# Batch 0 of a fused pooled-attention and feed-forward kernel: other PSUM banks for four steps, and one step earlier in TensorE's queue

## The chip, the cores and the metric

The kernel runs on one core of one Trainium2 chip. The metric is the time of one execution on the device in microseconds; 291.48 us is the median of three executions of the kernel before (291.36 to 291.85). One more execution was taken with the hardware profiler, and all rows below come from it.

## The reference, cut to what matters

```python
batch, n_heads, seq, head_dim = (8, 8, 576, 64)      # q, k, v
k_p = k.reshape(B, H, Sp, pool, D).mean(axis=3)      # pool = 8, Sp = 72
v_p = v.reshape(B, H, Sp, pool, D).mean(axis=3)
scores = scale * np.matmul(q, k_p.transpose(0, 1, 3, 2))
attn = np.exp(scores - max) / (sum + 1e-09)
attn_out = np.matmul(attn, v_p)
x = attn_out.transpose(0, 2, 1, 3).reshape(B * S, H * D)   # 4608 x 512
h = x @ w_in                                               # 512 x 2048
out = (h * np.cos(h)) @ w_out                              # 2048 x 512
```

Attention over keys and values pooled by eight, and behind it a feed-forward layer whose activation is h cos(h).

## The kernel before, in words

The work goes through nine chunks of 512 tokens (`TILE`). Each of the eight batches has 576 tokens: 512 make the chunk of the batch, and the last 64 of every batch together make the ninth chunk. For each chunk the feed-forward part multiplies by `w_in` (`up_mm`, L357), takes the cosine on ScalarE (`up_g`, L364), multiplies on VectorE (L367) and multiplies by `w_out` (`down_mm`, L370). The attention of batch b + 1 is worked in between the matmuls of the down-projection of chunk b. Batch 0 has nothing to hide behind: its attention is the prologue of the kernel, from L495 to L538, and this is what the diff changes.

PSUM is laid out by hand: three tiles `banks[0]` to `banks[2]` of two banks each (a bank is 512 float32 columns of 128 partitions) and two tiles `obanks[0]` and `obanks[1]` of one bank each. Every engine works through its own instructions in the order in which the program writes them (`manual_schedule`), and waits on semaphores where it reads what another engine writes, or writes what another still reads. These waits are made for whole banks: a read of columns 256 to 511 waits for an earlier write to columns 0 to 255 of the same bank.

The steps of batch 0, with the lines under which the profile lists them:

- `pool_k_mm` (L180) pools k by matmuls with the 0/1 matrix `groups`; copies L186 put the result into `kk`.
- `q_transpose_mm` (L240) transposes q in blocks; copies L241 put it into `qT`.
- `scores` is `scores_mm` (L260) and `scores_exp` (L270). A unit `us[i]` is 256 tokens by 4 heads: us[0] and us[1] are the two token halves for heads 0 to 3, us[2] and us[3] for heads 4 to 7. `REST` is the last 64 tokens for all heads, "the last columns".
- `sums_mm` (L289) sums the exponentials over keys by matmuls with `ones`; `inverse` is a logarithm (L304) and an exponential of its negative (L305) on ScalarE.
- `pool_v_mm` (L196) pools v of four heads; its `put` (L205) copies the result into `vz` on VectorE.
- `values_mm` (L298) multiplies pooled v by a unit's exponentials; `x_mul` (L312) multiplies the result by the inverse sums into `xT`, which `up_mm` reads. The first eight `up_mm` matmuls need heads 0 to 3 only, the next eight heads 4 to 7.
- `warm_up` (L487) is matmuls on constant data whose result nobody reads.

v of batch 0 comes in two transfers of 288 KB as bfloat16, heads 0 to 3 and heads 4 to 7, started by GpSimd at 3.03 and 3.84 us; q, k and the weights come by the same queue. ScalarE's work for this batch ends with the exponentials of `REST` (L270, `ex_rest`), and then it loads the tables for the cosine (L348).

Of the kernel before, what the change touches and what calls it, by code (L numbers as in the profile page):

```python
# [19 lines left out]
def kernel(  # L20
# [9 lines left out]
    nc = tc.nc  # L30
    B, H, S, D = q.shape
    Sp = S // POOL
# [14 lines left out]
    REST = (SEG[2], (0, H))  # L47
# [29 lines left out]
    banks = [psum.tile([128, 2, 512], FP32, name=f"bank{i}") for i in range(3)]  # L77
    obanks = [psum.tile([128, 512], FP32, name=f"obank{i}") for i in range(2)]
# [70 lines left out]
    def v_part(b):  # L149
        return vz[b % 2][:, :, 0:4:3, :]  # L150
# [39 lines left out]
    def pool_v_mm(b, pair, j0, j1):  # L190
        vb = staged["v", b]
        n = (j1 - j0) * D
        ps = pair if isinstance(pair, tuple) else (pair[:, 0, :], pair[:, 1, :])
        for t in range(ROW):
            for hp, rows in enumerate(half):
                nc.tensor.matmul(ps[hp][:Sp, 0:n], lhsT=groups[rows, t, :], rhs=vb[rows, j0:j1, t, :],  # L196
                                 start=(t == 0), stop=(t == ROW - 1))
        dst = v_part(b)[:, j0:j1].rearrange("p j a d -> p a j d")

        def put():  # L200
            parts = [(dst[:, a], p[:Sp, 0:n]) for a, p in enumerate(ps)]
            if not isinstance(pair, tuple):
                parts = [(dst, pair[:Sp, :, 0:n])]
            for o, i in parts:
                nc.vector.tensor_copy(out=o, in_=i.rearrange("p (j d) -> p j d" if o is not dst else "p a (j d) -> p a j d", d=D))  # L205

        return put

# [15 lines left out]
    def qT_tile(b):  # L224
        att["qT", b] = asb.tile([128, QB, 128], BF16, name="qT", tag="qT")

    def q_flat(b):
        return staged["q", b].rearrange("p j t d -> p (j t d)")
# [5 lines left out]
    def q_transpose_mm(b, bank, g0, g1):  # L234

        if ("qT", b) not in att:
            qT_tile(b)
        ps = bank.bitcast(BF16)[:, 0:(g1 - g0) * 128].rearrange("p (g n) -> p g n", n=128)
        for g in range(g0, g1):
            nc.tensor.matmul(ps[:, g - g0, :], q_flat(b)[:, g * 128:(g + 1) * 128], identity, is_transpose=True)  # L240
        return lambda copy: copy(out=att["qT", b][:, g0:g1, :], in_=ps)  # L241

    def ex_col(u, i):

        (c0, n), (h0, nh) = u
        return (i // 2 % 2 * (nh // 2) + i // 4 * 2 + i % 2) * n

    def scores(b, u, pair):
        scores_mm(b, u, pair)
        scores_exp(b, u, pair)  # L250

    def scores_mm(b, u, pair):
        (c0, n), (h0, nh) = u

        for i in [i + 2 * a for k in range(0, nh, 4) for i in (k, k + 1) for a in range(2)]:
            bank, c = divmod(ex_col(u, i), nh * n // 2)
            pj, hp = divmod(h0 + i, 2)
            g, r = divmod(ROW * pj + ORDER[c0 // 64], 2)
            ps = pair[bank][:Sp, c:c + n] if isinstance(pair, tuple) else pair[:Sp, bank, c:c + n]
            nc.tensor.matmul(ps.rearrange("p (g n) -> p g n", n=64),  # L260
                             lhsT=kk[b % 2][half[r], h0 + i, 0:Sp],
                             rhs=att["qT", b][half[r], g:g + n // 64, hp * 64:hp * 64 + 64])

    def scores_exp(b, u, pair):
        (c0, n), (h0, nh) = u
        ex = ex_rest[b % 2] if u == REST else asb.tile([Sp, 4 * 256], BF16, name="ex", tag="ex", bufs=EX)
        w = nh * n // 2
        for src, c, m in ([(pair[:Sp, :, 0:w], 0, 2)] if not isinstance(pair, tuple) else
                          [(bank[:Sp, 0:w].unsqueeze(1), a * w, 1) for a, bank in enumerate(pair)]):
            nc.scalar.activation(out=ex[:, c:c + m * w].rearrange("p (a n) -> p a n", a=m), in_=src,  # L270
                                 func=ACTF.Exp, scale=scale / POOL)
        att["ex", b, u] = ex

    def token(b, c0):

        return b * TILE + c0 if c0 < TILE else B * TILE + b * 64

    def quads(u):

        (c0, n), (h0, nh) = u  # L280
        for i in range(nh):
            yield i, (h0 + i) // 4, slice((h0 + i) % 4 * 32, (h0 + i) % 4 * 32 + 32), slice(ex_col(u, i), ex_col(u, i) + n)

    def sums_mm(b, u, cs):

        ex = att["ex", b, u]
        q0 = u[1][0] // 4
        for i, q, rows, c in quads(u):
            nc.tensor.matmul(cs[rows, q - q0, :], lhsT=ones[:Sp, :], rhs=ex[:, c])  # L289

    def values_mm(b, u, ps):

        ex = att.pop(("ex", b, u))
        q0 = u[1][0] // 4
        for e in range(2):
            for i, q, rows, c in quads(u):
                pj, hp = divmod(u[1][0] + i, 2)
                nc.tensor.matmul(ps[rows, q - q0, e, :],  # L298
                                 lhsT=vz[b % 2][:, pj, 3 * hp, :].rearrange("p (d e) -> p e d", e=2)[:, e],
                                 rhs=ex[:, c])  # L300

    def inverse(cs, name, bufs):
        inv = asb.tile([128] + list(cs.shape[1:]), FP32, name=name, tag=name, bufs=bufs)
        nc.scalar.activation(out=inv, in_=cs, func=ACTF.Ln)  # L304
        nc.scalar.activation(out=inv, in_=inv, func=ACTF.Exp, scale=-1.0)  # L305
        return inv

    def x_mul(b, q, c0, ps, inv):

        n = ps.shape[3]  # L310
        c = token(b, c0)
        nc.vector.tensor_mul(out=xT[:, :, q, c:c + n], in0=ps[:, 0], in1=inv.unsqueeze(1).to_broadcast([128, 2, n]))  # L312
# [108 lines left out]
    def first_q(copy, t0, t1):  # L421
        copy(out=q01[:, t0 * D:t1 * D], in_=first[:, 1, t0 * D:t1 * D])
# [18 lines left out]
    groups = consts.tile([128, ROW, Sp], BF16, name="groups")  # L441
# [42 lines left out]
    def warm_up(n, bank):  # L484

        for i in range(n):
            nc.tensor.matmul(bank, lhsT=warm[:, 0:128], rhs=warm)  # L487

    vec, act = nc.vector.tensor_copy, nc.scalar.copy
    us = BY_HEADS  # L490

    def unit(bank):
        return bank.rearrange("p (q e n) -> p q e n", q=1, e=2)

    warm_up(8, banks[1][:, 0, :])  # L495
    puts = pool_k_mm(0, obanks, 0, 2)
    warm_up(2, banks[1][:, 0, :])
    first_q(act, 0, 7)
    first_q(vec, 7, 18)
    puts[0](vec)  # L500
    puts[1](act)
    q_transpose_mm(0, banks[2][:, 0, :], 5, 9)(act)
    q_transpose_mm(0, banks[0][:, 0, :], 0, 5)(vec)
    warm_up(2, banks[1][:, 0, :])
    scores(0, us[0], banks[0])
    scores(0, us[1], banks[1])
    for put in pool_k_mm(0, obanks, 2, 4):
        put(vec)
    s01 = banks[0][:, 0, :].rearrange("p (i n) -> p i n", i=2)
    sums_mm(0, us[0], s01[:, 0:1])  # L510
    puts = q_transpose_mm(0, banks[2][:, 0, :], 9, 14), q_transpose_mm(0, banks[2][:, 1, :], 14, 18)
    for put in puts:
        put(vec)
    sums_mm(0, us[1], s01[:, 1:2])
    inv01 = inverse(banks[0][:, 0, :], "inv", 1)
    warm_up(1, obanks[0])
    scores(0, us[2], banks[2])
    scores(0, us[3], banks[1])
    pool_v_mm(0, tuple(obanks), 0, 2)()
    for i in range(2):  # L520
        values_mm(0, us[i], unit(banks[0][:, i, :]))
    s23 = [ob[:, 256:512] for ob in obanks]
    sums_mm(0, us[2], s23[0].unsqueeze(1))
    put = pool_v_mm(0, banks[2], 2, 4)
    scores_mm(0, REST, tuple(obanks))
    x_mul(0, 0, 0, unit(banks[0][:, 0, :]), inv01[:, 0:256])
    put()
    x_mul(0, 0, 256, unit(banks[0][:, 1, :]), inv01[:, 256:512])
    sums_mm(0, us[3], s23[1].unsqueeze(1))
    for i in range(2):  # L530
        values_mm(0, us[2 + i], unit(banks[2][:, i, :]))
    for i in range(2):
        inv = inverse(s23[i], "inv_h", 2)
        x_mul(0, 1, 256 * i, unit(banks[2][:, i, :]), inv)
    scores_exp(0, REST, tuple(obanks))
    bk = banks
    up_mm(0, 0, 0, 2)
    up_mm(0, 1, 0, 2)  # L538
# [9 lines left out]
    for t in range(NT):  # L548
        b = t + 1
        bk = [banks[1], banks[0], banks[2]] if t == 1 else banks  # L550
        for fp in range(FFCH // 2):
            up_mm(t, fp, 2 if fp < 2 and t < 1 else 0)
            between = ()
            if t == 0:
                if fp == 6:
                    puts = q_transpose_mm(1, obanks[0], 0, 5), q_transpose_mm(1, obanks[1], 5, 9)
# [70 lines left out]
        elif b < B:  # L627
            us = BY_TOKENS
# [4 lines left out]
            d = 2 if t == 1 else 0  # L633
# [84 lines left out]
```

## Time and profile before

| | |
|---|---|
| median of three executions | 291.48 us |
| their range | 291.36 to 291.85 us |
| the profiled execution's own time | 291.54 us |
| its span, first to last instruction | 289.5 us |
| granted TensorE clock, mean over the span | 0.997 |
| TensorE (PE) busy | 278.9 us, 96% of the span |
| VectorE (DVE) busy | 170.5 us, 59% |
| ScalarE (ACT) busy | 142.7 us, 49% |
| GpSimd (POOL) busy | 145.5 us, 50% |
| first up-projection matmul (L357) starts | 15.69 us |

Times inside the profile count from the span's start. A row of a timeline has the start, the busy time, the engine, the line, the operation, what is written and read, shapes, and a count where several were merged; in square brackets stands how long the engine had been idle before it and what ended that. TensorE's matmuls overlap one another, and the end of each is modelled, so that a row's busy time reaches into the next row. Some matmul records are missing from the trace.

### The profile page before, as it was taken

What the parts mean: (1) busy time and instruction counts of PE and PEld (TensorE: products, weight loads), DVE (VectorE), ACT (ScalarE), POOL (GpSimd) and SP (SyncE); (2) the same over time, 40 slices, a digit from 0 to 9 for tenths busy, and PEclk for the clock granted to TensorE, in tenths of its full rate; (3) what the DMA queues carried; (4) which work ended last, traced back from release to release, by engine and by line L of the source; (5) the groups of instructions that cost most, each with busy time, mean ns of one, the idle gap of its engine ahead of it and who ended that gap; (6) DMA issues with size and microseconds to landing.
All of it is one profiled execution on the core that took longest, in us unless ns stands there. A gap on an engine that the chain in (4) does not pass through costs nothing.

```text
span 289.5 us, 4905 instructions
## 1 busy us (share of the span) xinstructions
PE 278.9 (96%) x1955; PEld 146.7 (51%) x1989; DVE 170.5 (59%) x231; ACT 142.7 (49%) x143; POOL 145.5 (50%) x121
## 2 busy tenths in 40 slices
PE   7899999999999999999999999999999999999994
PEld 3655544555554555555555545554555454445443
DVE  6467886664756564757375737583766467217621
ACT  4786634678056904691369326841676065016400
POOL 8546937999964696479544983698000000000000
PEclk9999999999999999999999999999999999999998
DMA  7999999789877978795879776965603510230033
GB/s 204 197 205 211 206 206 191 150 155 217 134 149 104 202 118 168 103 162 111 171 73 202 114 155 114 188 122 112 130 1 74 119 36 2 56 83 8 0 72 74
DMA packets 57158, 36.89 MB, mean 127 GB/s; under 512 B 36400, under 2 KB 50928, under 8 KB 57136
## 3 DMA queue, kind: packets, MB, share of 16 engines
q0 software_dynamic: 17104, 17.77, 37.9%
q1 hardware_dynamic: 39792, 18.69, 32.7%
q8 instruction: 15, 0.25, 0.3%
q10 hardware_dynamic: 240, 0.13, 0.2%
q14 instruction: 7, 0.06, 0.1%
HBM read 36.70 MB, written 9.44 MB: 159 GB/s over the span
## 4 chain that ended last, share of the span: by engine, by line
PE 90%; DVE 3%; ACT 2%; DMA 2%; issue 1%; SPq 0%; DVEq 0%
PE bank L357 40%; PE obank L370 25%; PE bank L370 7%; PE obank L376 5%; PE bank L260 3%; PE bank L329 3%; PE bank L376 2%; DVE g_sb L367 2%; DMA g_sb<-in_q_dram 2%; ACT cos L364 2%; PE bank L398 1%; ACT ex L270 1%; PE bank L298 1%; DVE qT L241 0%; PE bank L240 0%
## 5 line engine op out<-in xcount | busy, mean ns | idle before, releaser
L364 ACT ACTIVATE cos<-bank,half_pi 128x1024 f32<-128x1024 f32 x72 | 80.4, 1118 | 117.3 <-PE bank L357 116.1
L357 PE MATMUL bank<-xT,w_in_sb 128*128 128x512 bf16 x565 | 125.4, 379 | 0.6
L367 DVE TENSOR_TENSOR g_sb<-bank,cos 128x1024 bf16<-128x1024 f32 x72 | 88.1, 1224 | 49.8 <-ACT cos L364 49.7
L357 PEld LDWEIGHTS <-w_in_sb 128*128 128x128 bf16 x576 | 65.1, 113 | 59.0 <-issue 0.2
L370 PE MATMUL obank<-w_out_sb,g_sb 128*128 128x512 bf16 x346 | 82.5, 379 | 0.7 <-issue 0.2
L370 PEld LDWEIGHTS <-g_sb 128*128 128x128 bf16 x462 | 41.9, 97 | 45.9 <-issue 2.2
L161 POOL TENSOR_TENSOR kv_st<-kv_st 72x2048 f32<-72x2048 bf16 (+1 forms) x13 | 50.3, 3873 | 16.7 <-DMA kv_st<-in_k_dram 16.7
L383 DVE COPY o_sb<-obank 128x512 f32<-128x512 f32 x21 | 14.4, 690 | 31.5 <-PE obank L370 23.1
L270 ACT ACTIVATE ex<-bank 72x1024 bf16<-72x1024 f32 x32 | 30.4, 1019 | 4.8 <-PE bank L260 4.8
L164 POOL TENSOR_TENSOR kv_st<-kv_st 72x1024 f32<-72x1024 f32 (+1 forms) x13 | 29.2, 2250 | 0.9
L370 PE MATMUL bank<-w_out_sb,g_sb 128*128 128x512 bf16 x94 | 25.8, 379 | 1.0 <-issue 1.0
L333 DVE TENSOR_TENSOR x_r<-bank,inv_r 128x512 bf16<-128x512 f32 (+1 forms) x32 | 22.1, 689 | 1.3 <-DVE inv_r L330 0.3
L376 PE MATMUL obank<-w_out_sb,g_sb 64*128 64x512 bf16 x144 | 18.3, 376 | 0.0
L168 POOL TENSOR_TENSOR kp<-kv_st 72x512 bf16<-72x512 f32 (+1 forms) x14 | 16.1, 1170 | 0.5
L260 PE MATMUL bank<-qT,kk 64*72 64x256 bf16 (+1 forms) x184 | 12.9, 249 | 1.4 <-DVE qT L241 0.6
L376 PEld LDWEIGHTS <-g_sb 64*128 64x128 bf16 x196 | 9.8, 94 | 7.3
L260 PEld LDWEIGHTS <-kk 64*72 64x72 bf16 x192 | 8.4, 111 | 8.6 <-issue 3.9
L119 POOL DMA_DIRECT2D kv_st<-in_v_dram x15 | 9.7, 661 | 4.8 <-DVE vz L171 4.5
L329 PEld LDWEIGHTS <-ex 72*128 72x128 bf16 x192 | 8.7, 97 | 6.2 <-ACT ex L270 1.8
L330 DVE RECIPROCAL inv_r<-bank 128x8 f32<-128x8 f32 (+1 forms) x32 | 6.5, 202 | 8.0 <-PE bank L329 7.4
L385 DVE COPY o_sb<-obank 128x512 f32<-128x512 f32 x6 | 4.1, 691 | 11.9 <-PE obank L376 11.9
L544 POOL COPY gate<-kk 1x1 bf16<-1x1 bf16 x5 | 0.9, 176 | 20.3 <-DMA kk<-kp 20.3
(86 smaller groups left out, 166.2 us busy)
## 6 DMA issues: line engine op xcount, KB each, us to landing
out_dram<-o_sb SPq DMA_DIRECT2D x70, 128.0 KB, 2.4
q_b<-in_q_dram POOLq DMA_DIRECT2D x6, 576.0 KB, 8.8
kv_st<-in_k_dram POOLq DMA_DIRECT2D x6, 512.0 KB, 6.4
kv_st<-in_v_dram POOLq DMA_DIRECT2D x6, 512.0 KB, 10.0
w_in_sb<-in_moe_w_in_dram POOLq DMA_DIRECT2D x8, 256.0 KB, 10.6
w_out_sb<-in_moe_w_out_dram POOLq DMA_DIRECT2D x8, 256.0 KB, 10.1
kv_st<-in_k_dram POOLq DMA_DIRECT2D x3, 288.0 KB, 10.2
q_b<-in_q_dram POOLq DMA_DIRECT2D x3, 288.0 KB, 10.4
```

The costliest lines, as they stand in the source:

```text
L161: add(out=s, in0=x[:, :, 0:4, :], in1=x[:, :, 4:8, :], op=ADD)
L164: add(out=s[:, :, 0:2, :], in0=s[:, :, 0:2, :], in1=s[:, :, 2:4, :], op=ADD)
L168: add(out=kp[:, h0:h1, slot, :], in0=s[:, :, 0, :], in1=s[:, :, 1, :], op=ADD)
L260: nc.tensor.matmul(ps.rearrange("p (g n) -> p g n", n=64), lhsT=kk[b % 2][half[r], h0 + i, 0:Sp], rhs=att["qT", b][half[r], g:g + n // 64, ...
L270: nc.scalar.activation(out=ex[:, c:c + m * w].rearrange("p (a n) -> p a n", a=m), in_=src, func=ACTF.Exp, scale=scale / POOL)
L329: nc.tensor.matmul(out[:, o0:o0 + D + 1], lhsT=ex[:, c:c + 128], rhs=v1)
L333: nc.vector.tensor_mul(out=x[:m].rearrange("p e h d -> p h e d"), in0=vals, in1=scale_of)
L357: nc.tensor.matmul(h[:, j, :], lhsT=w_in_cols(ki, fc), rhs=xT[:, ki % 2, ki // 2, t * TILE:(t + 1) * TILE], start=(ki == 0), stop=(ki == K ...
L364: nc.scalar.activation(out=cos, in_=h, func=ACTF.Sin, bias=half_pi[:, :1])
L367: nc.vector.tensor_mul(out=g_sb[:, 2 * fp:2 * fp + 2, :], in0=h, in1=cos)
L370: nc.tensor.matmul(o, lhsT=g_sb[:, fc, ms * 128:(ms + 1) * 128], rhs=w_out_sb[fc // 4][:, fc % 4, :], start=(fc == 0), stop=(fc == FFCH - 1))
L376: nc.tensor.matmul(ps, lhsT=g_sb[rows, fc, ms * 128:(ms + 1) * 128], rhs=w_out_sb[fc // 4][rows, fc % 4, :], start=start, stop=stop)
```

## The change

Batch 0's prologue is rewritten with names for the three bank pairs: `one` is `banks[0]`, `two` is `banks[2]` and `three` is `banks[1]`. Against the kernel before:

- What stood in `banks[1]` until the first sums (warm-up, scores of us[1]) stands in `banks[2]`, and what stood in `banks[2]` (transposes of q) stands in `banks[1]`; likewise the scores of us[2] and us[3].
- The single warm-up matmul after the first inverse is gone.
- `pool_v_mm` for v's first half comes ahead of the scores of us[2] and us[3], and its copies behind them. It writes columns 0 to 127 of each of the two obanks, as before.
- v's second half goes to columns 128 to 255 of the two obanks, not to a bank pair, and is copied by two instructions instead of one.
- The scores of the last columns go to `two`, one half of the heads in each bank, instead of to the obanks; one exponential of 512 columns takes the place of two of 256. The matmuls stand between the first inverse of the second half and its values.
- The sums of us[2] and us[3] go to the two banks of `three` instead of columns 256 to 511 of the obanks; their values go to the obanks instead of `banks[2]`. Sums, inverse, values and product are now written for us[2] and then for us[3].

```diff
     def pool_v_mm(b, pair, j0, j1):
...
-        ps = pair if isinstance(pair, tuple) else (pair[:, 0, :], pair[:, 1, :])
...
-                nc.tensor.matmul(ps[hp][:Sp, 0:n], lhsT=groups[rows, t, :], rhs=vb[rows, j0:j1, t, :],
+                nc.tensor.matmul(pair[hp][:Sp, 0:n], lhsT=groups[rows, t, :], rhs=vb[rows, j0:j1, t, :],
...
         def put():
...
+            for hp in range(2):
+                nc.vector.tensor_copy(out=v_part(b)[:, j0:j1, hp],
+                                      in_=pair[hp][:Sp, 0:n].rearrange("p (j d) -> p j d", d=D))
...
+    one, two, three = banks[0], banks[2], banks[1]
...
     inv01 = inverse(one[:, 0, :], "inv", 1)
-    warm_up(1, obanks[0])
-    scores(0, us[2], banks[2])
-    scores(0, us[3], banks[1])
-    pool_v_mm(0, tuple(obanks), 0, 2)()
+    put = pool_v_mm(0, [ob[:, 0:128] for ob in obanks], 0, 2)
+    scores(0, us[2], three)
+    scores(0, us[3], two)
+    put()
     for i in range(2):
-        values_mm(0, us[i], unit(banks[0][:, i, :]))
-    s23 = [ob[:, 256:512] for ob in obanks]
-    sums_mm(0, us[2], s23[0].unsqueeze(1))
-    put = pool_v_mm(0, banks[2], 2, 4)
-    scores_mm(0, REST, tuple(obanks))
-    x_mul(0, 0, 0, unit(banks[0][:, 0, :]), inv01[:, 0:256])
+        values_mm(0, us[i], unit(one[:, i, :]))
+    put = pool_v_mm(0, [ob[:, 128:256] for ob in obanks], 2, 4)
+    x_mul(0, 0, 0, unit(one[:, 0, :]), inv01[:, 0:256])
     put()
-    x_mul(0, 0, 256, unit(banks[0][:, 1, :]), inv01[:, 256:512])
-    sums_mm(0, us[3], s23[1].unsqueeze(1))
+    x_mul(0, 0, 256, unit(one[:, 1, :]), inv01[:, 256:512])
     for i in range(2):
-        values_mm(0, us[2 + i], unit(banks[2][:, i, :]))
-    for i in range(2):
-        inv = inverse(s23[i], "inv_h", 2)
-        x_mul(0, 1, 256 * i, unit(banks[2][:, i, :]), inv)
-    scores_exp(0, REST, tuple(obanks))
+        sums_mm(0, us[2 + i], three[:, i, 0:256].unsqueeze(1))
+        inv = inverse(three[:, i, 0:256], "inv_h", 2)
+        if i == 0:
+            scores_mm(0, REST, two[:, :, 0:256])
+        values_mm(0, us[2 + i], unit(obanks[i]))
+        x_mul(0, 1, 256 * i, unit(obanks[i]), inv)
+    scores_exp(0, REST, two[:, :, 0:256])
```

More of the change, by code (lines that the diff above doesn't have):

```diff
@@ L192, in pool_v_mm @@
         n = (j1 - j0) * D
-        ps = pair if isinstance(pair, tuple) else (pair[:, 0, :], pair[:, 1, :])
         for t in range(ROW):
             for hp, rows in enumerate(half):
-                nc.tensor.matmul(ps[hp][:Sp, 0:n], lhsT=groups[rows, t, :], rhs=vb[rows, j0:j1, t, :],
+                nc.tensor.matmul(pair[hp][:Sp, 0:n], lhsT=groups[rows, t, :], rhs=vb[rows, j0:j1, t, :],
                                  start=(t == 0), stop=(t == ROW - 1))
-        dst = v_part(b)[:, j0:j1].rearrange("p j a d -> p a j d")
         def put():
[L201 to L205, printed above, removed]
+            for hp in range(2):
+                nc.vector.tensor_copy(out=v_part(b)[:, j0:j1, hp],
+                                      in_=pair[hp][:Sp, 0:n].rearrange("p (j d) -> p j d", d=D))
         return put
@@ L493, in unit @@
         return bank.rearrange("p (q e n) -> p q e n", q=1, e=2)
-    warm_up(8, banks[1][:, 0, :])
+    one, two, three = banks[0], banks[2], banks[1]
+    warm_up(8, two[:, 0, :])
     puts = pool_k_mm(0, obanks, 0, 2)
-    warm_up(2, banks[1][:, 0, :])
+    warm_up(2, two[:, 0, :])
     first_q(act, 0, 7)
@@ L501 @@
     puts[1](act)
[L502 to L506, printed above, removed]
+    q_transpose_mm(0, three[:, 0, :], 5, 9)(act)
+    q_transpose_mm(0, one[:, 0, :], 0, 5)(vec)
+    warm_up(2, two[:, 0, :])
+    scores(0, us[0], one)
+    scores(0, us[1], two)
     for put in pool_k_mm(0, obanks, 2, 4):
         put(vec)
-    s01 = banks[0][:, 0, :].rearrange("p (i n) -> p i n", i=2)
+    s01 = one[:, 0, :].rearrange("p (i n) -> p i n", i=2)
     sums_mm(0, us[0], s01[:, 0:1])
-    puts = q_transpose_mm(0, banks[2][:, 0, :], 9, 14), q_transpose_mm(0, banks[2][:, 1, :], 14, 18)
+    puts = q_transpose_mm(0, three[:, 0, :], 9, 14), q_transpose_mm(0, three[:, 1, :], 14, 18)
     for put in puts:
@@ L514 @@
     sums_mm(0, us[1], s01[:, 1:2])
-    inv01 = inverse(banks[0][:, 0, :], "inv", 1)
-    warm_up(1, obanks[0])
-    scores(0, us[2], banks[2])
-    scores(0, us[3], banks[1])
-    pool_v_mm(0, tuple(obanks), 0, 2)()
-    for i in range(2):
-        values_mm(0, us[i], unit(banks[0][:, i, :]))
-    s23 = [ob[:, 256:512] for ob in obanks]
-    sums_mm(0, us[2], s23[0].unsqueeze(1))
-    put = pool_v_mm(0, banks[2], 2, 4)
-    scores_mm(0, REST, tuple(obanks))
-    x_mul(0, 0, 0, unit(banks[0][:, 0, :]), inv01[:, 0:256])
+    inv01 = inverse(one[:, 0, :], "inv", 1)
+    put = pool_v_mm(0, [ob[:, 0:128] for ob in obanks], 0, 2)
+    scores(0, us[2], three)
+    scores(0, us[3], two)
+    put()
+    for i in range(2):
+        values_mm(0, us[i], unit(one[:, i, :]))
+    put = pool_v_mm(0, [ob[:, 128:256] for ob in obanks], 2, 4)
+    x_mul(0, 0, 0, unit(one[:, 0, :]), inv01[:, 0:256])
     put()
-    x_mul(0, 0, 256, unit(banks[0][:, 1, :]), inv01[:, 256:512])
-    sums_mm(0, us[3], s23[1].unsqueeze(1))
+    x_mul(0, 0, 256, unit(one[:, 1, :]), inv01[:, 256:512])
     for i in range(2):
-        values_mm(0, us[2 + i], unit(banks[2][:, i, :]))
-    for i in range(2):
-        inv = inverse(s23[i], "inv_h", 2)
-        x_mul(0, 1, 256 * i, unit(banks[2][:, i, :]), inv)
-    scores_exp(0, REST, tuple(obanks))
+        sums_mm(0, us[2 + i], three[:, i, 0:256].unsqueeze(1))
[5 more added lines that the diff above has]
+    scores_exp(0, REST, two[:, :, 0:256])
     bk = banks
```

## The prediction

> **What bounds the kernel now.** I read the page first, then the chain of waits for 7 to 16.2 us, then the timelines of TensorE, VectorE, ScalarE and GpSimd for the same stretch, and last the single instructions in narrow windows. The page says who is late over the whole kernel.
>
> ```profile
> span 289.5 us, 4905 instructions
> ...
> PE 90%; DVE 3%; ACT 2%; DMA 2%; issue 1%; SPq 0%; DVEq 0%
> ```
>
> TensorE holds 90% of the chain; the other engines hold it almost only at the start. From 15.69 us, the first up-projection matmul (L357), TensorE runs nearly without a gap to the end. The change lies wholly before that point, so its worth is how far that matmul moves, if nothing later becomes late. The chain of waits shows what sets it (start, us, what):
>
> ```profile
> 10.61 0.83 DVE qT L241 x2
> ...
> 11.48 0.42 PE bank L260 x4
> ...
> 11.93 1.94 ACT ex L270 x2
> ...
> 13.89 0.68 DVE xT L312
> ...
> 14.62 0.43 DVE vz L205
> ...
> 15.09 0.62 PE bank L298 x16
> 15.71 0.35 PE bank L357
> ```
>
> Call the four large score units u0 to u3. The chain goes from the q copies to the scores of u2, their exponentials, the first product, the copy of v's second half, the values of u2 and u3, and the first L357. TensorE's timeline (start, busy us, line, tiles) has the same stretch with what is off the chain:
>
> ```profile
> 10.60 0.39 PE L487 MATMUL obank<-warm 128*128 128x512 bf16 x1
> 11.48 0.63 PE L260 MATMUL bank<-qT,kk 64*72 64x256 bf16 x8 [0.49 <-DVE qT L241]
> 11.91 0.70 PE L196 MATMUL obank<-kv_st,groups 64*72 64x128 bf16 x18
> 12.96 0.81 PE L298 MATMUL bank<-ex,vz 72*32 72x256 bf16 x16 [0.35 <-ACT ex L270]
> ...
> 13.81 0.69 PE L196 MATMUL bank<-kv_st,groups 64*72 64x128 bf16 x18
> 14.34 0.30 PE L260 MATMUL obank<-qT,kk 64*72 64x64 bf16 x8
> ...
> 15.09 0.62 PE L298 MATMUL bank<-ex,vz 72*32 72x256 bf16 x16 [0.23 <-DVE vz L205]
> ```
>
> VectorE:
>
> ```profile
> 12.61 0.48 DVE L205 CAST vz<-obank 72x128 bf16<-72x128 f32 x2 [1.19 <-PE obank L196]
> 13.89 0.69 DVE L312 TENSOR_TENSOR xT<-bank,inv 128x512 bf16<-128x512 f32 x1 [0.79 <-ACT ex L270]
> 14.62 0.42 DVE L205 CAST vz<-bank 72x256 bf16<-72x256 f32 x1
> ```
>
> The page's chain blames an exponential for the first product at 13.89. In the code that product reads no exponential of u2 or u3: it waits for the sixteen value matmuls, which end at 12.96 + 0.81 = 13.77, and these wait for the v copies of 12.61 to 13.10. So the true chain is v pooled (11.91), copied, values, first product, copy of v's second half. ScalarE and GpSimd:
>
> ```profile
> 14.67 0.39 ACT L304 ACTIVATE inv_h<-obank 128x256 f32<-128x256 f32 x1 [0.81 <-PE obank L260]
> ```
>
> ```profile
> 11.37 0.71 POOL L130 DMA_DIRECT2D w_in_sb<-in_moe_w_in_dram  x1 [0.75 <-DMA kv_st<-in_v_dram]
> ```
>
> The logarithm of u2's sums waits until 14.67 for the last columns' scores, which share its bank: a false wait. The GpSimd row says when v's first half is there: its load, issued at 3.03, landed 8.04 later, at 11.08 (the second half at 12.48).
>
> **The change part by part.**
>
> *v's first half ahead of the scores.* It can start when v has landed. The second half of q landed at 9.61 and its first transposing matmul began at 9.69, so 0.08 later: 11.16, against 11.91. The banks are free (last kk copy 10.59) and TensorE is idle from about 10.45. The 18 matmuls take 0.70 to their last end, and 0.53 until the next instruction can start (13.81 to 14.34). What is queued behind that new DMA wait is the scores of u2 and u3: they start at 11.16 + 0.53 = 11.69, not 11.48. So u2's exponential goes from 11.93 to 12.14, and u3's ends at 14.07 instead of 13.86: a loss of 0.21 on that branch.
>
> *What it moves.* Copies at 11.16 + 0.70 = 11.86 to 12.34 (0.48 as at 12.61). The second value matmul began 0.055 after the second copy (13.154 after 13.099), so 12.39, and the sixteenth ended 0.62 after that: 13.02, against 13.77. The first product followed by 0.11: 13.13, against 13.89, so 0.76 earlier.
>
> *v's second half into the obanks, two copies instead of one.* Pooling starts at 12.85 (v landed 12.48), well before VectorE is free. From the start of the first product to the end of the second the trace has 15.63 - 13.89 = 1.74; two 128-column copies instead of one of 256 add 0.48 - 0.42 = 0.06. End of the second product: 13.13 + 1.74 + 0.06 = 14.93, second copy done at 13.13 + 0.73 + 0.48 = 14.34. The one copy before had an extra semaphore instruction ahead of it; without it both could be 0.1 earlier.
>
> *Last columns' scores into bank 2.* They now wait for u3's exponential, which reads that bank: 14.07 + 0.05 = 14.12 (0.05 as between the first two exponentials and the sums behind them). Queued behind are the values of u2. Eight such scores need 0.23 (14.34 to 14.57), so TensorE is free at 14.35, when the copies of v end as well.
>
> *Values and sums of u2, u3.* Values go into the obanks after 14.34 + 0.05 = 14.39. Groups of four column-tiled matmuls start 0.11 apart (rows at 15.10, 15.21, 15.32, 15.43). Values u2, sums u3, values u3 are five groups, the last at 14.39 + 4 x 0.11 = 14.83. From the last group to the first L357 the trace has 15.44 to 15.69, of which the last 0.05 is VectorE's release. So TensorE reaches L357 at 15.03 to 15.08, and VectorE allows it at 14.93 + 0.055 = 14.99. I take 15.04: **0.65 us earlier than 15.69**. Bounds: with the copies 0.1 earlier 14.93 (gain 0.76), with a second changeover of 0.2 between column tiles and wide tiles (as 13.61 to 13.81) 15.24 (gain 0.45).
>
> *What hides the rest.* No DMA is moved, so GpSimd's and SyncE's queues keep their order. The deleted warm-up stood in an idle stretch; the granted clock is 1.00 in 8 to 12 and in 12 to 16 us across idle gaps of 0.49 and 0.35 us, and the new gap is about 0.7. Were the clock to fall, the warm rows at 1.47 have the price: 0.43 a matmul instead of 0.216. Exchanged banks in the first part change no wait. The logarithm of u2 moves from 14.67 to about 13.98, behind u3's exponential. The one for u3 starts after its sums, about 14.94; its inverse ends 0.40 + 0.42 later, 15.76; the last product ends by 16.47. TensorE needs it at 15.04 + 1.72 = 16.76: 0.29 of cover. One exponential of 512 columns replaces two of 256: between 0.37 (256) and 1.02 (1024) I take 0.58, against 0.63 for the pair. It ends at 16.25, the table load (1.28) at 17.55, and the first cosine is due at 18.48 - 0.65 = 17.83: 0.28 of cover. w_in lands at 15.53, 16.78, 18.05 and is wanted at 16.76, 18.49, 18.92. Further on, the closest thing that doesn't follow TensorE is q's second half of batch 1, landed 34.07 and used 35.70. So the shift should last to the end.
>
> The rule against this: The Trainium skill, "TensorE: Matmul & The Clock Gate", section "Wait — 56ns, not 53.3ns?", has 55.6 ns from start to start at 128 columns, which would make the 18 matmuls 1.00 us instead of 0.53, move the exponentials 0.47 later still and cut the gain to about 0.18. The trace has two of them at once on the two row halves (28 ns each), and I go by the trace.
>
> **The sum.** The profiled execution took 291.54 us with a span of 289.5, so 2.04 lies around the span; the median is 291.48, 0.06 below. 291.48 - 0.65 = 290.83, said as 290.85.
>
> **Rivals.** *Same: the tail of TensorE's queue keeps the gain.* The last columns' scores still wait for an exponential, and everything after them is in order. From these scores to L357 the trace has 15.69 - 14.34 = 1.35, with idle time inside; if that repeats from 14.12, L357 starts at 15.47, a gain of 0.22: 291.26. For it: u3's exponential ends 0.21 later. Against: the idle 0.23 in it was for v's copy, which now is ready at the same moment.
>
> *Slower: v's first half lands late.* Everything now hangs on one load: L357 starts 15.04 - 11.08 = 3.96 after its landing. The gain is gone if it lands at 11.73, and over 0.2% is lost from 12.31; at 12.48, where the second half lands, L357 starts at 16.44: 292.23. For it: sixteen DMA engines are shared and the scores, which need no v, now stand behind it. Against: GpSimd issues it third in the same order, and no transfer ahead of it is moved.
>
> **How the numbers follow.** About 0.2% (0.58 us) is what a measurement of this kernel can tell from no change, and my gain is hardly more. The forecast as worked: 0.69, of which 0.53 beyond that bound and 0.16 within; the first rival 0.17; the slower one, with a wait that I don't see, 0.14. So faster 0.53, same 0.33, slower 0.14. The forecast's own range is 290.6 to 291.1; with the first rival and a part of the second, 290.5 to 291.8.
>
> **What would show it.** Right: the first L196 at about 11.16 and no matmul from 10.7 to there; u2's exponential at 12.14; first product at 13.13; the logarithm of u2 at about 14.0; first L357 at 15.0 to 15.1, TensorE without gaps behind it. Wrong: L357 after 15.3; a gap before the ninth L357 (last product late) or before the first cosine; L357 matmuls further apart than 0.216.

## The result, and the profile after

| | before | changed |
|---|---|---|
| median of 20 executions | 291.50 us (291.27 to 292.21) | 291.04 us (290.79 to 291.59) |
| ratio, 95% interval | | 0.9984 (0.9978 to 0.9990) |
| profiled execution, its span | 291.54 us, 289.5 us | 291.02 us, 288.9 us |
| first up-projection matmul (L357, now L353) | 15.69 us | 15.05 us |

The kernel became 0.46 us faster. That is 0.16%, a real gain by its interval, and smaller than the 0.58 us that the prediction named as the bound for a single measurement. The forecast was 0.65 us and 290.85.

The page of the changed kernel, its span, the busy time of the engines and the chain by engine:

```profile
span 288.9 us, 4935 instructions
...
PE 282.0 (98%) x1988; PEld 147.0 (51%) x1988; DVE 170.9 (59%) x232; ACT 142.8 (49%) x142; POOL 145.3 (50%) x121
...
PE 94%; DMA 3%; ACT 1%; POOL 1%; DVE 0%; issue 0%; POOLq 0%; DVEq 0%
```

VectorE's 3% of the chain is gone, and the DMA in it, 2% before and the load of q, is now another one, with 3%. (TensorE's busy time of 282.0 us isn't to be set against the 278.9 of before: here 1988 matmul records are there, there 1955.) The chain of waits of the changed kernel from 7 to 16.2 us (start, us, what) shows which:

```profile
3.03 8.13 DMA kv_st<-in_v_dram
11.15 0.04 issue
11.20 0.69 PE obank L195 x18
11.89 0.24 PE bank L256 x4
12.13 0.02 issue
12.15 1.94 ACT ex L266 x2
14.09 0.04 issue
14.13 0.33 PE bank L256 x8
14.46 0.33 PE obank L294 x8
14.79 0.11 PE bank L285 x4
14.90 0.22 PE obank L294 x8
15.12 1.20 PE bank L353 x5
```

The copies of q, the first product and the copies of v have left the chain. It now runs from the landing of v's first half to the pooling, through the scores queued behind it, two exponentials, the last columns' scores, whose bank the second exponential reads, and the last values. TensorE's timeline of the changed kernel has the same stretch:

```profile
10.47 0.29 PE L285 MATMUL bank<-ex,ones 72*32 72x256 bf16 x4
11.20 0.69 PE L195 MATMUL obank<-kv_st,groups 64*72 64x128 bf16 x18 [0.44 <-DMA kv_st<-in_v_dram]
11.73 0.60 PE L256 MATMUL bank<-qT,kk 64*72 64x256 bf16 x8
12.27 0.82 PE L294 MATMUL bank<-ex,vz 72*32 72x256 bf16 x16
13.01 0.69 PE L195 MATMUL obank<-kv_st,groups 64*72 64x128 bf16 x18
13.64 0.29 PE L285 MATMUL bank<-ex,ones 72*32 72x256 bf16 x4
14.13 0.33 PE L256 MATMUL bank<-qT,kk 64*72 64x64 bf16 x8 [0.20 <-ACT ex L266]
...
15.05 1.27 PE L353 MATMUL bank<-xT,w_in_sb 128*128 128x512 bf16 x5
```

Between the first pooling and the first L353 only one idle gap of TensorE is left that names a releaser, 0.20 us at 14.13; before, the same stretch had one of 0.35 and one of 0.23. VectorE of the changed kernel, with the first, second and last product:

```profile
13.20 0.69 DVE L308 TENSOR_TENSOR xT<-bank,inv 128x512 bf16<-128x512 f32 x1 [0.79 <-ACT ex L266]
...
14.20 0.68 DVE L308 TENSOR_TENSOR xT<-bank,inv 128x512 bf16<-128x512 f32 x1
...
15.83 0.69 DVE L308 TENSOR_TENSOR xT<-obank,inv_h 128x512 bf16<-128x512 f32 x1 [0.22 <-ACT inv_h L301]
```

and its ScalarE:

```profile
13.98 0.39 ACT L300 ACTIVATE inv_h<-bank 128x256 f32<-128x256 f32 x1
...
15.70 0.57 ACT L266 ACTIVATE ex_rest<-bank 72x512 bf16<-72x512 f32 x1
16.29 1.28 ACT L344 ACT_TABLE_LOAD   x1
17.87 1.12 ACT L360 ACTIVATE cos<-bank,half_pi 128x1024 f32<-128x1024 f32 x1 [0.30 <-PE bank L353]
```

The logarithm no longer waits for the last columns, and the first cosine starts at 17.87 instead of 18.48. Compared one by one, all 72 cosines of the kernel start 0.60 to 0.64 us earlier, and so does the last matmul (284.73 against 285.37). In these two profiles nothing was given back inside the kernel.

### The profile page after: what moved, and what is told of

Its sections match the earlier page's. It is cut to its first block, busy times and chain, and to the rows that moved or that the text cites. A ratio compares the mean times of both kernels' runs of the same rounds, so it can differ in the third digit from the quotient of the medians.

```text
span 288.9 us, 4935 instructions
## 1 busy us (share of the span) xinstructions
PE 282.0 (98%) x1988; PEld 147.0 (51%) x1988; DVE 170.9 (59%) x232; ACT 142.8 (49%) x142; POOL 145.3 (50%) x121
## 4 chain that ended last, share of the span: by engine, by line
PE 94%; DMA 3%; ACT 1%; POOL 1%; DVE 0%; issue 0%; POOLq 0%; DVEq 0%
PE bank L353 43%; PE obank L366 27%; PE bank L366 8%; PE obank L372 5%; PE bank L256 3%; DMA kv_st<-in_v_dram 3%; PE bank L325 3%; PE bank L372 2%; PE bank L394 1%; ACT ex L266 1%; PE bank L294 0%; POOL kv_st L89 0%; PE obank L195 0%; PE bank L285 0%; DVE kk L215 0%
## 5 line engine op out<-in xcount | busy, mean ns | idle before, releaser
L353 PE MATMUL bank<-xT,w_in_sb 128*128 128x512 bf16 x576 | 126.0, 379 | 0.0
L353 PEld LDWEIGHTS <-w_in_sb 128*128 128x128 bf16 x576 | 65.1, 113 | 59.0 <-DMA w_in_sb<-in_moe_w_in_dram 0.2
L366 PE MATMUL obank<-w_out_sb,g_sb 128*128 128x512 bf16 x360 | 83.9, 379 | 0.0
L366 PE MATMUL bank<-w_out_sb,g_sb 128*128 128x512 bf16 x102 | 27.6, 380 | 0.0
```

Of the source, the lines that this page charges most:

```text
L353: nc.tensor.matmul(h[:, j, :], lhsT=w_in_cols(ki, fc), rhs=xT[:, ki % 2, ki // 2, t * TILE:(t + 1) * TILE], start=(ki == 0), stop=(ki == K ...
L366: nc.tensor.matmul(o, lhsT=g_sb[:, fc, ms * 128:(ms + 1) * 128], rhs=w_out_sb[fc // 4][:, fc % 4, :], start=(fc == 0), stop=(fc == FFCH - 1))
```

## The experiments

The question left by the result was not whether the prologue became shorter, but which part did it and why the time moved less than the prologue. My theory: the order (v pooled ahead of the scores) starts the gain, the banks alone bring nothing, and both together are worth what the rows show; what is missing in the time lies outside the span. Rivals: the deleted warm-up brings or costs something by itself; a limit other than v's landing sets the first L353; the missing part is measurement scatter.

The experiments came in three groups with 35, 33 and 32 runs of the kernel before beside them, whose medians were 291.57, 291.54 and 291.55. The table gives the median over all runs of a kernel, the ratio to before with its interval, and means of three quantities: the time, the span, and the difference of the two. In some runs of `e2_banks` and `e4_v_swapped` TensorE's clock fell, and one run of `e10_nowarm` took 293.46; these runs are left out of the means of time and span and are told of below.

| kernel | median us | ratio (95%) | mean time | mean span | outside the span | VectorE rows |
|---|---|---|---|---|---|---|
| before (100 runs) | | | 291.61 | 289.63 | 1.98 | 231 |
| changed (32 runs: 20 above, 12 of `r1_after`) | 291.02 | | 291.09 | 288.95 | 2.13 | 232 |
| `r1_after` alone | 290.99 | 0.9981 (0.9972 to 0.9989) | 291.04 | 288.90 | 2.14 | 232 |
| `e1_order` | 291.11 | 0.9985 (0.9974 to 0.9995) | 291.17 | 289.21 | 1.97 | 231 |
| `e2_banks` | 291.94 | 1.0025 (1.0001 to 1.0049) | 291.88 | 289.74 | 2.14 | 232 |
| `e2w_banks_warm` | 291.74 | 1.0006 (0.9998 to 1.0015) | 291.76 | 289.61 | 2.15 | 232 |
| `e3_warm` | 291.17 | 0.9981 (0.9972 to 0.9989) | 291.10 | 288.95 | 2.15 | 232 |
| `e4_v_swapped` | 292.91 | 1.0064 (1.0034 to 1.0095) | 292.18 | 290.03 | 2.14 | 232 |
| `e5_v_free` | 290.84 | 0.9978 (0.9969 to 0.9987) | 290.96 | 288.81 | 2.15 | 232 |
| `c6_rest` | 290.95 | 0.9979 (0.9970 to 0.9988) | 291.01 | 288.87 | 2.14 | 232 |
| `e10_nowarm` | 291.81 | 1.0008 (0.9996 to 1.0020) | 291.67 | 289.67 | 2.00 | 231 |
| `p8_act3` | 291.14 | 0.9983 (0.9974 to 0.9991) | 291.12 | 288.98 | 2.14 | 232 |
| `p9_dve1` | 290.94 | 0.9976 (0.9966 to 0.9986) | 290.94 | 288.98 | 1.97 | 231 |
| `c7_best` | 291.05 | 0.9977 (0.9969 to 0.9986) | 290.95 | 288.96 | 1.99 | 231 |

The standard error of a mean time or span is about 0.02 for before, 0.05 for the changed kernel, and 0.04 to 0.14 for the others; that of the part outside the span is 0.01 to 0.04.

### The changed kernel again: `r1_after`

No edit.

> The changed kernel once more, so that the experiments have it on the same chip. My theory (v's first half, pooled 0.7 us earlier, carries the whole chain up to the first up-projection matmul): that matmul at 15.0 to 15.1 us in the profile, time 0.45 to 0.65 us below the kernel before. If the smaller difference of the medians (0.46) is the true one and the 0.64 of the profile was luck, the profile of another execution shows it at 15.2 or later.

TensorE's timeline:

```profile
10.86 0.69 PE L195 MATMUL obank<-kv_st,groups 64*72 64x128 bf16 x18 [0.38 <-DMA kv_st<-in_v_dram]
...
14.71 1.70 PE L353 MATMUL bank<-xT,w_in_sb 128*128 128x512 bf16 x7
```

The profiled run had v's first half at 10.81 us and the first L353 at 14.71, 3.90 after it; the profile after has 11.15 and 15.05, also 3.90, and so has the profile of `p9_dve1`, a kernel with the same prologue (11.26 and 15.15). Two profiles of one kernel differ by 0.34 in where the prologue ends, and the whole difference is the landing. That is the slower rival's mechanism at work in small. It doesn't hold in every run: in the profiles of `e3_warm` and `p8_act3` the first L353 came 4.59 and 4.49 after the landing; there the scores of us[2] started at 12.16 and 12.02 us, and in `p8_act3` they waited for the copies of q and not for v (last section).

### The order alone: `e1_order`

The kernel before, with its old banks, and only this moved (the lone warm-up is gone too):

```diff
-    warm_up(1, obanks[0])
+    put = pool_v_mm(0, tuple(obanks), 0, 2)
     scores(0, us[2], banks[2])
     scores(0, us[3], banks[1])
-    pool_v_mm(0, tuple(obanks), 0, 2)()
+    put()
```

> The kernel before with one thing moved: v's first half is pooled ahead of the scores of the second head group, its copies behind them, and the lone warm-up is gone; all banks as before. Theory (the order carries the gain): first product at 13.2 us instead of 13.89. But v's second half still goes into the bank pair that the third unit's exponential reads, and stands behind that unit's sums, so its pooling can't start before 13.4, its copy not before 14.1, and the second product ends at 15.17: first up-projection matmul at about 15.2, time 0.45 us below the kernel before, 0.15 above the changed kernel. Rival (the banks carry it): first up-projection matmul at 15.6 or later, time within 0.15 us of the kernel before.

The mean span falls by 0.42 (289.63 to 289.21), 0.26 short of the changed kernel's 288.95. With a standard error of 0.14 the means alone don't settle that; the trace shows the same amount at a place. (One run of the twelve took 292.37; without it the mean span would be 289.09.) TensorE of `e1_order`:

```profile
12.50 0.82 PE L298 MATMUL bank<-ex,vz 72*32 72x256 bf16 x16
13.46 0.29 PE L289 MATMUL obank<-ex,ones 72*32 72x256 bf16 x4
13.68 0.69 PE L196 MATMUL bank<-kv_st,groups 64*72 64x128 bf16 x18
...
15.55 0.81 PE L357 MATMUL bank<-xT,w_in_sb 128*128 128x512 bf16 x3
```

and its VectorE:

```profile
13.43 0.69 DVE L312 TENSOR_TENSOR xT<-bank,inv 128x512 bf16<-128x512 f32 x1 [0.79 <-ACT ex L270]
14.48 0.42 DVE L205 CAST vz<-bank 72x256 bf16<-72x256 f32 x1 [0.36 <-PE bank L196]
```

With the old banks the pooling of v's second half stands behind the sums of us[2], which wait for an exponential. It starts at 13.68, although v had landed at 12.84, and VectorE idles 0.36 us for it. The first L357 comes 15.55 - 11.39 = 4.16 after v's landing instead of 3.90: the 0.26 again. It stands at 15.55 and not at the expected 15.2 because v landed 0.31 later in this run than in the profile before.

### The banks alone: `e2_banks` and `e2w_banks_warm`

`e2_banks` is the changed kernel with the old place of the pooling and no warm-up:

```diff
-    put = pool_v_mm(0, [ob[:, 0:128] for ob in obanks], 0, 2)
     scores(0, us[2], three)
     scores(0, us[3], two)
-    put()
+    pool_v_mm(0, [ob[:, 0:128] for ob in obanks], 0, 2)()
```

> The changed kernel with the order undone alone: v's first half is pooled behind the scores again; all new banks stay. Theory (order): pooling at 11.95, first product at 13.9, two copies instead of one, second product ends at 15.6; first up-projection matmul at 15.65 to 15.75, time within 0.1 us of the kernel before. Rival (banks): first up-projection matmul at 15.2 or earlier, time 0.3 us or more below the kernel before.

`e2w_banks_warm` has `warm_up(1, obanks[0])` ahead of these scores as well, as the kernel before has it:

> The kernel with the new banks and the old order, now with the lone warm-up matmul in its old place. Without it this kernel was 0.37 us slower than the kernel before in the median, and in its profile the granted clock fell to 0.50 at 11.95 us for 10.2 us. Theory A (the lost warm-up is all of it: without it and with nothing pooled in that gap, TensorE is too idle): no clock of 0.50 after the start, time within 0.1 us of the kernel before. Theory B (the new banks cost by themselves in the old order, through two copies where there was one and a longer tail of column-tiled matmuls): still 0.25 us or more above the kernel before, first up-projection matmul 15.9 or later.

With the warm-up the banks alone change the span by nothing: 289.61 against 289.63. Nor do they help in time: 291.76 against 291.61. The 0.15 us lie outside the span (below). So the other banks are worth something only together with the order: they take away the wait that the order makes next (the row at 13.68 above). Without the warm-up the undisturbed runs took 291.88, 0.27 more than before and not within the expected 0.1; 0.16 of it lie outside the span, and the other 0.11 have an error of 0.07. Without the warm-up two of eleven runs took 295.83 and 296.32, and the profiled one is among them. Its windows of 4 us:

```profile
core 0: us, PE busy (x) PEld busy (x) DVE busy (x) ACT busy (x) POOL busy (x), PEclk, DMA share, GB/s
4.00:8.00 4.00, 3.70 (x57) 1.88 (x57) 2.60 (x9) 2.37 (x5) 3.92 (x7) 1.00 1.10 232
8.00:12.00 4.00, 2.28 (x61) 1.60 (x57) 2.03 (x6) 2.54 (x4) 1.69 (x3) 0.99 1.19 196
12.00:16.00 4.00, 3.61 (x50) 2.78 (x51) 0.73 (x4) 2.55 (x3) 1.98 (x3) 0.50 1.23 201
16.00:20.00 4.00, 4.00 (x52) 2.14 (x47) 2.92 (x6) 2.48 (x6) 1.94 (x4) 0.50 1.24 205
20.00:24.00 4.00, 4.00 (x15) 1.64 (x13) 0.00 (x0) 1.74 (x2) 1.62 (x4) 0.73 1.18 207
```

The granted clock is 1.00, then 0.50 from 11.95 for 10.2 us, then 1.00 again, and the run is some 4 us longer than the undisturbed ones. In 8 to 12 us TensorE is busy 2.28 of 4 us. Its idle gaps there are 0.59, 0.44 and 0.76 us, none long in itself. None of the eleven runs of `e2w_banks_warm` was disturbed, but two of eleven against none of eleven is too little to say that the warm-up prevents it.

### The warm-up alone: `e3_warm` and `e10_nowarm`

`e3_warm` is the changed kernel with the warm-up back in its place; `e10_nowarm` is the kernel before with that one line deleted.

```diff
     inv01 = inverse(...)
+    warm_up(1, obanks[0])        # e3_warm
-    warm_up(1, obanks[0])        # e10_nowarm
```

> The changed kernel with the lone warm-up matmul put back, ahead of v's first half and on the first obank. Theory: it ends before v lands (11.1 us), so nothing moves: within 0.1 us of the changed kernel, first up-projection matmul at 15.0 to 15.1. Rival (the warm-up held the clock, and its loss cost a part of the gain): 0.15 us or more below the changed kernel.

> The kernel before with the lone warm-up matmul taken out and nothing else. Theory (in the old order that matmul held the clock, and pooling v in the same gap does so in the new order): TensorE is idle from 10.7 to 11.5 us, in some executions the granted clock falls to 0.50 for 10.2 us as it did in the kernel with the new banks and the old order, and these take 3.5 to 4.5 us more; the others stay within 0.1 us of the kernel before. Rival (the fall came from the new banks): no execution above 292.5 us, no clock of 0.50 in the profile after the first 8 us.

In the changed kernel the warm-up makes no difference: spans 288.95 and 288.95, times 291.10 and 291.09. In the kernel before, its deletion gives a ratio whose interval holds 1, and without the run of 293.46 a mean of 291.67 against 291.61. So the deleted matmul brought none of the gain. In the profile its place is one long idle gap, without a fall of the clock:

```profile
12.06 0.63 PE L260 MATMUL bank<-qT,kk 64*72 64x256 bf16 x8 [0.81 <-DVE qT L241]
```

The run of 293.46 had a mean clock of 0.994; whether the clock fell there for a short time is open, since the profile is of another run, and another kernel's run with 0.994 took 292.37.

### v's halves in the other order: `e4_v_swapped`

The changed kernel, with v's halves loaded in the other order, so that the half that the pooling needs comes second:

```diff
     load_even(staged["q", 0], 0, q, 2, 4)
-    load_even(staged["v", 0], 0, v, 0, 2)
     load_even(staged["v", 0], 0, v, 2, 4)
+    load_even(staged["v", 0], 0, v, 0, 2)
```

> The changed kernel with the loads of v's two halves issued in the other order, so that the first half lands about 1.4 us later (12.5 instead of 11.1). Theory (one landing carries the chain, 3.9 us ahead of the first up-projection matmul): that matmul at 16.3 to 16.5, time 1.3 us above the changed kernel, 0.7 to 0.9 above the kernel before. Rival (scores and exponentials set the end as much as v): less than 0.7 us above the changed kernel.

Six runs took 292.06 to 292.31, mean 292.18, 1.09 more than the changed kernel and 0.57 more than before: the slower rival, with a landing about as late as its last example (12.62 in the profiled run, 12.48 there). The prediction gave 292.23 for that, but the agreement is in part luck: the mean span is only 0.40 longer than before, where the working had 0.75, and 0.16 lie outside the span. In the other six the clock fell as well, and they took 293.52 to 296.40. The profiled run is one of them; TensorE's timeline:

```profile
12.66 1.18 PE L195 MATMUL obank<-kv_st,groups 64*72 64x128 bf16 x18 [1.99 <-DMA kv_st<-in_v_dram]
13.63 1.06 PE L256 MATMUL bank<-qT,kk 64*72 64x256 bf16 x8
```

Here the gap is one piece of 1.99 us, and the matmuls behind it last almost twice as long as in the changed kernel (1.18 against 0.69, 1.06 against 0.60).

### v's landing taken away: `e5_v_free`

The first pooling reads the staged k, which lies there long before, in place of v:

```diff
-        vb = staged["v", b]
+        vb = staged["k" if j0 == 0 else "v", b]
```

> The changed kernel, but the first pooling reads k's data in place of v's, which are there at 8.2 us, so that nothing waits for v's first half (heads 0 to 3 of batch 0 get pooled k as values). Theory: pooling starts at 10.75, behind the kk copies; the scores wait for the q copies again (11.6), the last exponential ends at 13.95, and the path through it, the last columns' scores and the values comes to the first up-projection matmul at 14.9: only 0.15 us gained, since that path is next in line. Rival (the wait for v is most of what is left): 14.4 or earlier, 0.5 us or more gained.

TensorE's timeline:

```profile
10.51 0.70 PE L195 MATMUL obank<-kv_st,groups 64*72 64x128 bf16 x18
11.40 0.63 PE L256 MATMUL bank<-qT,kk 64*72 64x256 bf16 x8 [0.19 <-DVE qT L237]
...
13.83 0.33 PE L256 MATMUL bank<-qT,kk 64*72 64x64 bf16 x8 [0.40 <-ACT ex L266]
...
14.75 1.05 PE L353 MATMUL bank<-xT,w_in_sb 128*128 128x512 bf16 x3
```

Against the profile after, the pooling moves up by 0.69, but the first L353 only by 0.30, and q's second half landed 0.40 earlier in this profile by itself; the mean span falls by 0.14, with an error of 0.10. Now the scores wait for the copies of q again, and the last columns' scores wait 0.40 for the exponential. On average v's landing is the limit by no more than about that; the branch of scores and exponentials lies close behind it.

### The last columns' scores out of the way: `c6_rest`

The changed kernel, with these scores in a bank that is free earlier, and the sums ahead of the values:

```diff
+    scores_mm(0, REST, three[:, :, 256:512])
+    for i in range(2):
+        sums_mm(0, us[2 + i], (three, two)[i][:, 0, 0:256].unsqueeze(1))
+        invs.append(inverse((three, two)[i][:, 0, 0:256], "inv_h", 2))
     for i in range(2):
-        sums_mm(0, us[2 + i], three[:, i, 0:256].unsqueeze(1))
-        inv = inverse(three[:, i, 0:256], "inv_h", 2)
-        if i == 0:
-            scores_mm(0, REST, two[:, :, 0:256])
         values_mm(0, us[2 + i], unit(obanks[i]))
```

> The changed kernel with the last columns' scores in the free columns of the bank pair whose exponential ends first, so that they run ahead of the sums and don't wait for the last exponential; the sums of the fourth unit go to the other pair and stand ahead of the values. Theory: TensorE has four groups of column-tiled matmuls behind v's last copy instead of five and no wait in between: first up-projection matmul 3.75 to 3.8 us after v lands instead of 3.9, now held by VectorE's second product as much; time 0.1 us below the changed kernel, which five rounds hardly tell. Rival (VectorE alone sets it): 3.85 or more.

TensorE's timeline:

```profile
11.23 0.69 PE L195 MATMUL obank<-kv_st,groups 64*72 64x128 bf16 x18 [0.53 <-DMA kv_st<-in_v_dram]
...
13.58 0.30 PE L256 MATMUL bank<-qT,kk 64*72 64x64 bf16 x8
13.80 0.66 PE L285 MATMUL bank<-ex,ones 72*32 72x256 bf16 x8
14.28 0.71 PE L294 MATMUL obank<-ex,vz 72*32 72x256 bf16 x16
14.97 0.81 PE L353 MATMUL bank<-xT,w_in_sb 128*128 128x512 bf16 x2
```

The last columns' scores now start at 13.58 and wait for nothing, and the first L353 comes 14.97 - 11.19 = 3.78 after the landing instead of 3.90. Half of the 0.26 that these scores had held in the chain came back in another place: the sums of us[3] now wait for the same exponential. The mean span is 0.08 shorter than the changed kernel's, about as much as the error of that difference, so a gain is likely from the rows but not shown by the times. The profile of `c7_best` below, which has the same rearrangement, also has 3.78.

### What lies outside the span: `p8_act3`, `p9_dve1`, `c7_best`

The table's last but one column has two groups. Before and `e1_order` have 1.97 to 1.98 us between the span and the time; every kernel with the new banks up to `c6_rest` has 2.13 to 2.15. These two groups also differ in the number of instructions: the new text has one instruction more on VectorE (two copies of v's second half instead of one) and three fewer on ScalarE (245 and 242 records in the traces with the waits among them; the page's rows, which leave waits out, have 143 and 142). Two kernels undo one of these each, without a touch on the prologue's chain:

```diff
+    spare = consts.tile([1, 4], BF16, name="spare")           # p8_act3
+    for i in range(3):
+        nc.scalar.copy(out=spare[:, i:i + 1], in_=staged["k", 0][0:1, 0, 0, i:i + 1])
...
-    nc.vector.memset(half_pi, math.pi / 2.0)                  # p9_dve1
+    nc.gpsimd.memset(half_pi, math.pi / 2.0)
```

> The changed kernel with three one-element copies more on ScalarE at 5.2 us, where it is idle, so that its program has as many instructions as before the change (three more than after it). So far the time that lies outside the span is 1.98 us in the mean for the kernel before and for the one with the order alone, and 2.13 to 2.15 for every kernel with the new banks, whose ScalarE programs are three instructions shorter and VectorE programs one longer. Theory (length of ScalarE's program): outside the span 1.95 to 2.00, time 0.15 us below the changed kernel (290.85). Rival (VectorE's, or neither): 2.13 to 2.15 outside, time as the changed kernel.

> The changed kernel with one memset moved from VectorE to GpSimd, so that VectorE's program has as many instructions as before the change. Theory (length of VectorE's program): outside the span 1.95 to 2.00, time 0.15 us below the changed kernel. Rival (ScalarE's, or neither): 2.13 to 2.15, time as the changed kernel, or up to 0.1 more since the weights' loads are issued 0.1 us later.

> The kernel with the last columns' scores ahead of the last exponential (four groups behind v's last copy), with both program lengths brought back to those of the kernel before. Theory: first up-projection matmul 3.75 to 3.8 us after v's first half lands, outside the span 1.95 to 2.00, time 290.75 to 290.85, below the changed kernel and the kernel before. Rival (what lies outside the span has another cause): 2.14 outside, 290.95.

`c7_best` is `c6_rest` with both edits. The pages' rows of busy time and instructions, of before:

```profile
PE 278.9 (96%) x1955; PEld 146.7 (51%) x1989; DVE 170.5 (59%) x231; ACT 142.7 (49%) x143; POOL 145.5 (50%) x121
```

of `p8_act3`:

```profile
PE 279.4 (97%) x1954; PEld 147.1 (51%) x1988; DVE 170.5 (59%) x232; ACT 143.0 (49%) x145; POOL 145.5 (50%) x121
```

and of `p9_dve1`:

```profile
PE 279.2 (97%) x1954; PEld 147.0 (51%) x1988; DVE 170.8 (59%) x231; ACT 142.7 (49%) x142; POOL 145.5 (50%) x122
```

ScalarE's three instructions back: 2.14, no change. VectorE's one instruction away: 1.97, as before, with the changed kernel's span (288.98). `c7_best`, also with 231 on VectorE, has 1.99. Thirteen kernels divide without an exception: 231 rows on VectorE and 1.97 to 2.00, 232 rows and 2.13 to 2.15. So the count on VectorE goes with the 0.16 us, and ScalarE's doesn't; nor does GpSimd's, which is 121 in before and 122 in `p9_dve1`. Why an instruction on VectorE should cost this much outside the span isn't shown: the kernels with 231 also scatter more (standard deviation 0.08 to 0.10 from run to run, against 0.03 to 0.04), so it may be something that the length of the program brings in or out of step. No kernel had 230 or 233, and only the memset was moved away.

`p9_dve1` and `c7_best` have the lowest mean times of the versions that do the whole work (`e5_v_free` doesn't), 290.94 and 290.95 against 291.09 of the changed kernel; the difference of 0.14 has an error of 0.11, so that it is the part outside the span that shows it (0.16 with an error of 0.04 for `p9_dve1`), not the times. `c7_best` missed its expected 290.75 to 290.85. The two don't differ measurably from each other, so the rearrangement of `c6_rest` on top isn't worth keeping on this evidence.

## Why the prediction was right, and where it was not

**The gain in the prologue was right, step by step.** The first pooling started at 11.20 (forecast 11.16, the landing being 0.07 later than assumed), the exponential of us[2] at 12.15 (12.14), the first product at 13.20 (13.13), the logarithm of us[2] at 13.98 (about 13.98), the last columns' scores at 14.13 (14.12), the first L353 at 15.05 (15.04). That the last agrees to 0.01 is in part luck, since it moves with v's landing: `r1_after` has it at 14.71. Counted from the landing the forecast had 15.04 - 11.08 = 3.96, and three profiles have 3.90. Eighteen pooling matmuls took 11.726 - 11.196 = 0.53 us until the next instruction, as the prediction took from the trace. They start in pairs, one for each row half, 3 to 4 ns apart, and from pair to pair it is 56 ns (11.391, 11.395, then 11.447 us). An estimate by 55.6 ns for every matmul (The Trainium skill, "TensorE: Matmul & The Clock Gate", section "Wait — 56ns, not 53.3ns?") would have been 1.00 us; in this trace that figure fits the pair, not the single matmul. The mean span fell by 289.63 - 288.95 = 0.68, with an error of 0.06, for the 0.65 worked out.

**The term that was mis-sized is the 2.04 us around the span.** The sum took it over unchanged. By the means it went from 1.98 to 2.13, and these 0.16 us (by unrounded means) are what separates the 0.68 of the span from the measured difference of the mean times, 291.61 - 291.09 = 0.52, where 0.65 was forecast. The changed kernel with VectorE's count restored, `p9_dve1`, is 291.61 - 290.94 = 0.67 faster than before, with an error of 0.10: the gain as worked out. In the prediction's own terms the result lies below its bound of 0.58 us for telling a change from none; that the change is real, the many runs tell. The prediction priced the second copy of v at 0.06 us in VectorE's timeline and saw no other cost of it.

**The first rival (the tail of TensorE's queue keeps the gain) fell.** Its premise held to 0.01 us, its price didn't: behind the 14.13 there is no idle time, and L353 comes 0.92 after it, not 1.35. The profiles of `r1_after`, `e3_warm`, `e5_v_free`, `p8_act3` and `p9_dve1` have the same 0.92 from these scores to L353.

**The second rival (v lands late) didn't occur and is real.** `r1_after` shows the start of L353 follow a landing 0.34 earlier by the same amount, and `e4_v_swapped` is slower than before. Its price was too high, though: with v's halves swapped, 1.36 us apart in the profile after, the span grew by 290.03 - 288.95 = 1.08, not by as much as the landing. Where the rest went is open, since the profiled run is one with a fallen clock. What the rival left out is that the longer gap can also cost the clock: half of those runs lost another 1.3 to 4.2 us.

**The clock.** The prediction argued from gaps of 0.49 and 0.35 us that one of 0.7 would do no harm, and had only a price per matmul for a fall. In the changed kernel it did no harm in 32 runs, and the gap was 0.44. But the reason was too weak, since the length of one gap doesn't decide: the clock fell in `e2_banks` with three gaps of 0.59, 0.44 and 0.76 in one stretch, and held in the profile of `e10_nowarm` with one of 0.81.

**The cover.** The working listed w_in's pieces from 15.53 on and left out the piece that the first L353 itself needs. It landed at 14.87 in the profile after, 0.18 ahead of that matmul (0.42 in `r1_after`): a thin cover which held, and which any further gain here would have to look at first. The other two covers held: the ninth L353 started at 16.805, behind a last product that ended at 16.52, and the first cosine waited for TensorE, the table load having ended at 17.57.

**Whose gain it was.** The order alone gives 0.42 of the 0.68 in the span, the banks alone nothing, the deleted warm-up nothing; the remaining 0.26 is the banks' on top of the order, by a wait that the trace of `e1_order` shows; the means alone, with errors of 0.14 and 0.15 on these two parts, don't tell them apart.

## What to carry to other kernels

Work out a gain in the prologue from the rows of the stretch itself, down to which wait ends last, and then compare the mean spans of many runs as well as the times: here the span showed the forecast gain and the time showed three quarters of it. When one change has two parts, look for the wait that the first makes and the second removes; alone, the second can be worth nothing. Before a matmul that nobody reads is deleted, look at all idle stretches of TensorE in the few microseconds around it, not only at the one gap that it stood in: the clock fell here where three short gaps came together.

## What the runs showed of the hardware that was not expected

**Several short gaps can cost TensorE its clock.** The trace's record of the granted clock goes by steps of 3.413 us: the half clock lasted 10.24 us in `e2_banks` and `e4_v_swapped` (three steps), the first stretch at full clock 6.83 us (two), and an undisturbed run has 283.31 us at full clock (83) or 279.89 (82). Counted in these steps, with the matmul records that are there, TensorE was busy in 56% of the step before the fall in `e2_banks` (8.54 to 11.95) and in 51% of it in `e4_v_swapped` (8.72 to 12.13). The Trainium skill, "TensorE: Matmul & The Clock Gate", section "What's actually happening", has a free-running window of 3413 ns, as the steps here show, and half the clock after at least one idle window. By the measurement the step before a fall needn't be idle, and 1.99 us was the longest gap. How much work holds the clock isn't shown. The busy share alone doesn't decide it: at the end of the same two profiles, steps with 46% and 44% (from 288.43 and 288.61 us) were not followed by a fall, which came a step later, while steps with 39% and less at the end of other kernels were. The steps before the two falls hold a transposing of q, and those at the end hold none. If these transposes are left out of the count, the two steps have 38% and 34%, every step before a fall has 39% or less, and every other step at full clock 44% or more. This is a fit made afterwards to fourteen profiles, and no run tests it.

**Where the window falls is a matter of the run.** The full clock began between 4.42 and 7.45 us in the fourteen profiles. This fits what only some runs of a kernel showed, the fall in 2 of 11 and in 6 of 12: it may depend on where the gap lies in the window, which no run tests. A late full clock also goes with a late prologue: in the three profiles in which it came after 7 us (7.21, 7.37, 7.45), warm-up matmuls were still 0.40 us apart at 6.4, where others had 0.23, and the scores of us[2] stood at 12.02 to 12.16. I didn't separate how much of the scatter of some 0.2 us between runs this is.

**The time around the span is not a constant.** It was about 1.98 or 2.14 us, and went with a single instruction on VectorE far from the end of the kernel. The cause is open.
